# Moving the folded-row sums of a Fourier-and-mixer kernel: three batches' steps put into other slots

## The chip, the cores and the metric

The kernel runs on one core of one Trainium2 chip. The metric is the device time of one execution in microseconds. TensorE (PE) does the matrix products, VectorE (DVE) and ScalarE (ACT) do elementwise work and read PSUM, GpSimd (POOL) does small copies and gathers, SyncE (SP) issues most transfers.

## The reference

For `x` of shape (8, 3136, 256), in float32:

```python
X = np.fft.fft(x, axis=1)
X = np.fft.fft(X, axis=2)
x = X.real                                  # the first part

xt = x.transpose(0, 2, 1)                   # the second part
h  = xt @ U @ V                             # U: 3136 x 32, V: 32 x 3136
u  = x + h.transpose(0, 2, 1)
ch = np.maximum(u @ w_ch1, 0.0) @ w_ch2     # 256 -> 1024 -> 256
out = u + ch
```

So each batch of 3136 rows goes through a two-dimensional Fourier transform, of which the real part is kept, then a rank-32 mix along the rows, then a two-layer product along the columns, with the residual added.

## The kernel before

**Two streams of work.** The transform of a batch works on folded rows: by the symmetries of sine and cosine, rows (and columns) are added to and subtracted from their mirror images first, and the products then need only a quarter of the terms. The second part works on chunks of 512 rows out of the first half of each batch (1568 rows; eight batches make 25 chunks, `c` from 0 to 24) together with their mirror rows (`hf` 1). While the chunks of one batch go through the second part, the next batch is transformed, and the one after that is folded. Batch 0 is transformed at the start, in an order written out by hand.

**The fold of a batch** (`fold`, all on VectorE through `fold_tt`, line 453 in the profile) has these steps: for the even and then the odd quarters, `along_d` adds and subtracts columns of the forward rows (`eof` from the loaded `xf`) and of the reversed rows (`eor` from `xr`), in two parts each; `load_part` then loads the next batch into `xf` and `xr` (two gathers issued by GpSimd, one transfer by SP, and small ones); `mirror` sums the two into `eos`, in two parts. At the end `half` and `fourth` make `ge`, `gc` (even rows) and `go` (odd rows), which the products read. Batch 1 has 13 steps, batches 2 to 6 have 17, batch 7 has 15. GpSimd copies two columns beside them (`alone`).

**The transform of a batch** (`transform`) has these steps, each of them products on TensorE and what reads them: `a` and `s` are the even rows (`even_rows`: a first product, a ScalarE copy `ev`, a second product into the same PSUM tile, ScalarE copies into A or B, then VectorE's `mirrored`, line 635); `c` and `d` are the odd rows (`seq`: the first product is copied to `ev` by ScalarE and halved into `eh` by VectorE; the second is joined with `eh` by VectorE in `join`, lines 584 to 598, into A or B). In the text `a0`, `a1`, `c0` and so on are the first and second of each. Types `a`, `c` make A, types `s`, `d` make B. `chan` multiplies A and B along the columns and copies the result into S (`h` 0) or T (`h` 1); `lowrank`, `hidden` and `spread_rank` make the rank-32 factors.

**The chunks.** In chunk `c`, `direct` multiplies `u` by the first weights (four tiles `p1` at a time, ScalarE's activations of line 845), `mirrors` turns the same tiles into those of the mirror rows (line 861), `second_product` multiplies by the second weights into a tile `p2` and VectorE adds `u` (lines 923, 924), `store` writes `o` out, and `front` makes the next `u`: two small products `ph` and two VectorE sums with S and T (line 458), then a transposing transfer on SP. `odd_part` makes `uo`.

**PSUM.** The tiles `p1` have four buffers, `p2` two, and all of the transform's tiles and the two `ph` of a front share the two buffers with the tag `dft`.

**What sets the order.** A chunk has places called slots, numbered 6c + 0 to 6c + 5 with some in between (4.5, 4.75). `turn(c, sl)` runs the steps that are due there. `put` fills the table: for each batch, first the fold's steps at the slots in `FOLDS` (or at `mid` - 18 + n), and then the transform's steps from slot `mid` on, one list for each slot. `mid` is 11 for batch 1, 23 for batch 2, and 39, 57, 75, 93, 111 for batches 3 to 7. Products and folds are pinned to program order among themselves; joins, copies and `o` sums are placed by the scheduler's own estimate of the times. Line 1145 puts the seventh list of batch 1 at slot 16.5.

Of the kernel before, what the change touches and what calls it, by code (L numbers as in the profile page):

```python
# [31 lines left out]
def kernel(  # L32
# [9 lines left out]
    nc = tc.nc  # L42
    B, S, D = x.shape
# [413 lines left out]
    def in_turn(c, *a, **k):  # L457
        ins = nc.vector.tensor_tensor(*a, **k)  # L458
        if pinned and c <= 2:
            tc.keep_in_program_order(ins)  # L460

    def mm(*a, **k):
        ins = nc.tensor.matmul(*a, **k)  # L463
        if len(pinned) > 1:
            tc.keep_in_program_order(ins)
        if pinned:
            pinned.append(ins)
# [185 lines left out]
        nc.scalar.copy(ST[b]["tab"][:, typ, 0, :].rearrange("p (g r) -> p g r", r=R),  # L653
                       four(kept["pt"][:], typ * R))

    def chan(b, ch, h, tag="dft"):
        d = ST[b]
        at, n0 = ((0, 0), (785, 1), (393, 786), (1177, 785))[ch]
        n = 393 if ch == 0 else 392
        if b == 0 and ch == 2:  # L660
            at, n0, n = 392, 784, 393
        pt = psum.tile([P, TE], FP32, tag=tag, name="pst", bufs=BUFS[tag])
        mm(pt[:, :n], MC[:, h * P:(h + 1) * P], d["A"][:, at:at + n], start=True, stop=False)
        mm(pt[:, :n], (MSX if ch == 3 and b == 0 else MSN)[:, h * P:(h + 1) * P], d["B"][:, at:at + n],
           start=False, stop=True)
        to = d["ST"[h]][:, n0:n0 + 2 * n - 1:2]
        if b == 0 and h == 1:
            nc.vector.tensor_copy(to, pt[:, :n])
        else:
            nc.scalar.copy(to, pt[:, :n])  # L670

    def lowrank(b):
        d = ST[b]
# [78 lines left out]
    def spread_rank(b):  # L752

        (nc.scalar if b == 1 else nc.sync).dma_start_transpose(out=QF[b % 2][:], in_=QT[:])

    def width(c):
        return min(CH, NCOL - c * CH)

    def pieces(c):

        cuts = []
        r = c * CH
        while r < c * CH + width(c):
            b, n = divmod(r, HALF)
            end = min(c * CH + width(c) - b * HALF, HALF)
            cuts.append((b, n, end, r - c * CH))
            r = b * HALF + end
        return cuts
# [3 lines left out]
    def front(c, hf):  # L772

        k = CK.setdefault(c, {})
        first = hf == 1 and c in DIRECT
        u = cp.tile([P, 2 * CH // P + first, P], BF16, tag="ut1" if first else f"u{hf}", name=f"u{hf}",
                    bufs=2 if first else 2 - hf)
        u = k["u", hf] = u[:, 0:2 * CH // P].rearrange("p (s t) m -> p s (t m)", s=2)
        phs = [psum.tile([P, CH], FP32, tag="dft", name="ph", bufs=BUFS["dft"]) for s in range(2)]
        w = width(c)  # L780
        if w < CH:
            nc.gpsimd.memset(u[:, :, w:].bitcast(I32), 0)
        for b, lo, hi, col in pieces(c):
            at, v = (w - col - hi + lo, S - hi + 1) if hf else (col, lo)
            for s in range(2):
                rows = slice((2 * hf + s) * R, (2 * hf + s + 1) * R)
                mm(phs[s][:, at:at + hi - lo], TA[b % 2][rows, s * P:(s + 1) * P], VV[rows, v:v + hi - lo],
                   start=True, stop=True)
        for s in range(2):
            for b, lo, hi, col in pieces(c):  # L790
                src = ST[b]["S" if s == hf else "T"]
                if hf == 0:
                    at, src = col, src[:, lo:hi]
                else:
                    at = w - col - hi + lo
                    if lo == 0:
                        nc.vector.tensor_tensor(u[:, s, w - col - 1:w - col], phs[s][:, w - col - 1:w - col],
                                                src[:, HALF:HALF + 1], op=AL.add)
                        lo = 1
                    src = src[:, hi - 1:lo - 1:-1] if lo else src[:, hi - 1::-1]  # L800
                in_turn(c, u[:, s, at:at + hi - lo], phs[s][:, at:at + hi - lo], src, op=AL.add)
        if hf == 1:
            for b, lo, hi, col in pieces(c):
                if lo == 0:
                    nc.gpsimd.tensor_copy(UH[:, :, b], u[:, :, w - col - 1])
                    nc.gpsimd.tensor_copy(UH[0:1, :, b], u[0:1, ::-1, w - col - 1])
        else:
            if w < CH:
                nc.gpsimd.tensor_copy(u[:, :, w:w + B], UH[:])
        if c in DIRECT:  # L810
            return
        n = CH // P
        ut = k["ut", hf] = cp.tile([P, 2 * n + 1, P], BF16, tag=f"ut{hf}", name=f"ut{hf}", bufs=2)
        nc.gpsimd.memset(ut[:, 2 * n, 0:2], 0.0)
        nc.sync.dma_start_transpose(out=ut[:, 0:2 * n], in_=u.rearrange("p s r -> p (s r)"))
        fx = k["fx", hf] = cp.tile([P, n, 2], FP32, tag=f"fx{hf}", name=f"fx{hf}", bufs=2)
        if hf:
            nc.gpsimd.tensor_tensor(fx[:, :, 0], ut[:, n:2 * n, 0], ut[:, 0:n, 0], op=AL.subtract)
        nc.gpsimd.tensor_tensor(fx[:, :, 1], ut[:, 0:n, 0] if hf else ut[:, n:2 * n, 0],  # L819
                                ut[:, n + 1:2 * n + 1, 0], op=AL.subtract)  # L820
# [109 lines left out]
    def transform(b):  # L930

        def odd_rows(typ, pn):
            seq(b, 1, typ, pn)
            if pn:
                join(b, 1, typ)

        def even(typ, pn):
            even_rows(b, typ, pn)
            if pn:
                mirrored(b, typ, ST[b])  # L940

        a = [lambda pn=pn: even(1, pn) for pn in range(2)]
        s = [lambda pn=pn: even(0, pn) for pn in range(2)]
        c = [lambda pn=pn: odd_rows(1, pn) for pn in range(2)]
        d = [lambda pn=pn: odd_rows(0, pn) for pn in range(2)]
        rank = [lambda: lowrank(b)]
        ch = [lambda ch=ch, h=h: chan(b, ch, h) for ch in range(2) for h in range(2)]
        q = [lambda: hidden(b)]
        if b == 1:
            return 11, [a[:1], c[:1] + a[1:], c[1:] + s[:1], s[1:] + d[:1], d[1:] + ch[:1], ch[1:3],  # L950
                        rank + ch[3:] + q + [lambda: spread_rank(b)]]
        if b == 2:
            return 23, [a[:1], a[1:] + c[:1], [], c[1:] + s[:1], s[1:], d[:1], d[1:], ch[:1], ch[1:2] + rank,
                        q, ch[2:3], ch[3:]]
        return 6 * (b * HALF // CH) - 15, [[x] for x in a + c + d[:1] + s + d[1:] + ch[:1] + rank + ch[1:2] + q + ch[2:]]
# [173 lines left out]
    def put(slot, *steps):  # L1129
        due.setdefault(slot, []).extend(steps)  # L1130

    FOLDS = {1: (5, 5, 6, 6, 6, 7, 8, 8, 9, 9, 10, 10, 12),
             2: (15, 15, 15, 16, 16, 17, 17, 18, 18, 19, 20, 20, 21, 21, 21, 22, 22.75),
             3: (27, 27, 29, 30, 30, 31, 31, 32, 33, 33, 34, 34, 35, 35, 36, 37, 38)}
    for b in range(1, B):
        mid, steps = transform(b)
        todo = list(fold(b))
        places_ = FOLDS.get(b) or [mid - 18 + n for n in
                                   ((1, 2, 3, 5, 5, 6, 6, 8, 9, 10, 11, 11, 12, 13, 14, 15, 17) if b + 1 < B else
                                    (1, 2, 3, 5, 6, 6, 8, 9, 10, 11, 12, 13, 14, 15, 17))]  # L1140
        assert len(todo) == len(places_)
        for step, at in zip(todo, places_):
            put(at, step)
        for n, step in enumerate(steps):
            put(16.5 if mid + n == 17 and b == 1 else mid + n, *step)
# [4 lines left out]
    def turn(c, sl):  # L1150
        for step in due.get(6 * c + sl, []):
            step()
# [30 lines left out]
    for c in range(1, NCH):  # L1183
        direct(c, 0)
        if c > 1:
            odd_part(c)
        turn(c, 0)
        second_product(c - 1, 0, 2, between=lambda: turn(c, 1))
        store(c - 1, 0)
        mirrors(c, 0)  # L1190
        front(c, 1)
        second_product(c - 1, 1, 0)
        turn(c, 2)
        direct(c, 1)
        turn(c, 3)
        second_product(c - 1, 1, 2, between=lambda: turn(c, 4))
        store(c - 1, 1)
        turn(c, 4.5)
        mirrors(c, 1)
        if c + 1 < NCH:  # L1200
            front(c + 1, 0)
        turn(c, 4.75)
        second_product(c, 0, 0)
        turn(c, 5)
# [38 lines left out]
```

## Time and profile before

| | us |
|---|---|
| median of 3 runs | 442.1 (442.1 to 442.47) |
| the profiled execution | 441.79 |
| its span, first to last instruction | 440.0 |
| TensorE busy | 422.8 (96%) |
| VectorE busy | 318.6 (72%) |
| ScalarE busy | 293.0 (67%) |
| GpSimd busy | 136.2 (31%) |

In the rows of a timeline the first number is the start in us from the span's start, the second how long it took, then engine, line, operation, the tile written and the tiles read, their shapes, and how many instructions are merged. A bracket at the end gives the idle time of that engine just before, and who ended it. Matrix products are pipelined, so neighbours overlap by some 0.15 us. All products stand on line 463, all folds on line 453, since helpers issue them.

### The profile page before, as it was taken

To read this page: it belongs to the slowest core of one execution; us is meant where nothing else is said; L and a number is where in the kernel's file an instruction comes from. 1 tells how busy PE (TensorE), PEld (TensorE's weight loads), DVE (VectorE), ACT (ScalarE), POOL (GpSimd) and SP (SyncE) were. 2 spreads that over 40 slices of the span, in tenths; PEclk is the share of its full clock that TensorE was granted. 3 is DMA by queue.
4 is the path that set the end of the run, shared out by engine and by line. 5 is a ranking of instruction groups with operands and counts; after the bars stand their busy time and mean duration, and the time that the engine had idled before them with its cause. 6 is when DMAs were issued, how large, how long until landed. Compare 5 with 4: busy or idle time off the path is not lost.

```text
span 440.0 us, 9349 instructions
## 1 busy us (share of the span) xinstructions
PE 422.8 (96%) x3457; PEld 283.9 (65%) x3504; DVE 318.6 (72%) x663; ACT 293.0 (67%) x635; POOL 136.2 (31%) x340
## 2 busy tenths in 40 slices
PE   5989999999999999999999999999999999999996
PEld 2764666666666666667666666667666766666675
DVE  8988985997799778759867778769867554353442
ACT  7958765666667757766667757766667757765651
POOL 8871331571214144423253232332132100111111
PEclk9999999999999999999999999999999999999999
DMA  7898698479399766925886386776234423434544
GB/s 194 215 224 191 153 276 107 132 217 243 101 199 255 118 153 177 252 73 151 197 168 203 101 208 74 184 188 134 65 97 126 114 75 95 103 113 127 121 119 125
DMA packets 89166, 67.83 MB, mean 154 GB/s; under 512 B 55403, under 2 KB 82431, under 8 KB 89119
## 3 DMA queue, kind: packets, MB, share of 16 engines
q1 hardware_dynamic: 83350, 52.79, 50.0%
q0 software_dynamic: 5472, 14.36, 12.8%
q8 instruction: 27, 0.44, 0.4%
q14 instruction: 21, 0.16, 0.1%
q10 hardware_dynamic: 296, 0.07, 0.1%
HBM read 28.86 MB, written 25.69 MB: 124 GB/s over the span
## 4 chain that ended last, share of the span: by engine, by line
PE 80%; ACT 7%; DVE 6%; DMA 2%; POOL 2%; issue 2%; SPq 1%; ACTq 0%
PE p L463 65%; PE pt L463 7%; PE pst L463 4%; ACT h L845 3%; PE ph L463 2%; DMA xr<-in_x_dram 2%; DVE eos L453 1%; PE ptt L463 1%; ACT h L861 1%; ACT S L670 1%; DVE B L584 1%; PE pq L463 1%; DVE B L590 1%; ACT ev L616 1%; SPq L87 1%
## 5 line engine op out<-in xcount | busy, mean ns | idle before, releaser
L463 PE MATMUL p<-w,h 128*128 128x256 bf16 x1576 | 195.1, 273 | 0.0
L463 PEld LDWEIGHTS <-h 128*128 128x128 bf16 x1576 | 148.7, 98 | 40.5 <-issue 16.5
L861 ACT ACTIVATE h<-p 128x512 bf16<-128x512 f32 (+1 forms) x200 | 101.5, 595 | 83.1 <-PE p L463 77.8
L845 ACT ACTIVATE h<-p 128x512 bf16<-128x512 f32 (+1 forms) x200 | 101.8, 600 | 8.5 <-PE p L463 8.0
L928 POOL TENSOR_TENSOR o<-o,fx 128x2 f32<-128x2 f32 (+1 forms) x95 | 48.3, 508 | 151.4 <-DVE o L924 83.7
L463 PE MATMUL p<-u,w 128*128 128x512 bf16 (+1 forms) x354 | 90.4, 374 | 3.0 <-ACT u L725 0.5
L923 DVE TENSOR_TENSOR o<-p,ut 128x256 f32<-128x256 f32 (+1 forms) x95 | 39.6, 416 | 64.4 <-PE p L463 44.1
L463 PEld LDWEIGHTS <-w 128*128 128x128 bf16 x512 | 41.8, 97 | 38.1 <-issue 1.8
L463 PE MATMUL p<-uo,wd 128*128 128x512 bf16 (+1 forms) x199 | 50.6, 375 | 0.3
L57 POOL DMA_INDIRECT xf<-in_x_dram,xidx x32 | 37.0, 1157 | 20.5 <-DVE eof L453 10.3
L458 DVE TENSOR_TENSOR u<-ph,T 128x512 bf16<-128x512 f32 (+23 forms) x63 | 34.3, 555 | 10.2 <-PE ph L463 8.2
L924 DVE TENSOR_TENSOR o<-p,ut 128x256 f32<-128x256 f32 (+1 forms) x95 | 38.8, 409 | 0.0
L453 DVE TENSOR_TENSOR eof<-xf 99x1016 bf16<-99x1016 f32 (+1 forms) x33 | 38.2, 1170 | 0.8 <-DMA xf<-in_x_dram,xidx 0.8
L453 DVE TENSOR_TENSOR eor<-xr 99x1016 bf16<-99x1016 f32 (+1 forms) x34 | 38.4, 1141 | 0.0
L458 DVE TENSOR_TENSOR u<-ph,S 128x512 bf16<-128x512 f32 (+23 forms) x63 | 34.2, 553 | 1.3 <-PE ph L463 0.8
L819 POOL TENSOR_TENSOR fx<-ut 128x4 f32<-128x4 bf16 x48 | 14.7, 306 | 49.8 <-DMA ut<-u 49.7
L463 PEld LDWEIGHTS <-wd 128*128 128x128 bf16 x200 | 19.4, 98 | 13.1 <-issue 0.4
L463 PE MATMUL pt<-te,gc 98*128 98x229 bf16 (+1 forms) x192 | 24.0, 260 | 0.7 <-ACT ev L616 0.5
L670 ACT CAST S<-pst 128x392 bf16<-128x392 f32 (+1 forms) x30 | 18.6, 621 | 6.7 <-PE pst L463 6.4
L463 PEld LDWEIGHTS <-gc 98*128 98x128 bf16 x216 | 19.4, 97 | 5.1 <-issue 1.1
L463 PE MATMUL ph<-vv,ta 32*128 32x512 bf16 (+15 forms) x126 | 20.4, 324 | 1.6 <-DVE tab L598 0.8
L670 ACT CAST T<-pst 128x392 bf16<-128x392 f32 (+1 forms) x28 | 17.3, 617 | 6.9 <-PE pst L463 6.8
(178 smaller groups left out, 446.6 us busy)
## 6 DMA issues: line engine op xcount, KB each, us to landing
out_dram<-o SPq DMA_DIRECT2D x33, 512.0 KB
xr<-in_x_dram SPq DMA_DIRECT2D x15, 784.0 KB
out_dram<-o SPq DMA_DIRECT2D x8, 384.0 KB
out_dram<-o SPq DMA_DIRECT2D x8, 256.0 KB
out_dram<-o SPq DMA_DIRECT2D x10, 128.0 KB
xr<-in_x_dram SPq DMA_DIRECT2D x2, 392.0 KB
ut<-u SPq DMA_TRANSPOSE x48
vv<-vv SPq DMA_DIRECT2D x3, 196.0 KB
```

The source lines that it names most:

```text
L57: nc.gpsimd.indirect_dma_start(out_, None, bass.AP(t.tensor, t.offset, [[w, rows], [1, w]]), bass.IndirectOffsetOnAxis(idx, 0), element_of ...
L87: return [lambda dst=dst, dims=dims, at=at: (eng or nc.sync).dma_start(out=dst, in_=bass.AP(t.tensor, lo + at, dims)) for dst, dims, at in ...
L453: ins = nc.vector.tensor_tensor(*a, **k)
L458: ins = nc.vector.tensor_tensor(*a, **k)
L463: ins = nc.tensor.matmul(*a, **k)
L670: nc.scalar.copy(to, pt[:, :n])
L819: nc.gpsimd.tensor_tensor(fx[:, :, 1], ut[:, 0:n, 0] if hf else ut[:, n:2 * n, 0], ut[:, n + 1:2 * n + 1, 0], op=AL.subtract)
L845: nc.scalar.activation(k["h", 0][q][:, j - 4 * q, :w], p1[:, :w], AF.Relu)
L861: nc.scalar.activation(k["h", 1][q][:, g, :w], k["p1"][g][:, :w][:, ::-1], AF.Relu)
L923: nc.vector.tensor_tensor(o[:, ts, 0:P], p2[:, :w, 0:P], ut[:rows, ts, 0:P], op=AL.add)
L924: nc.vector.tensor_tensor(o[:, ts, P:D], p2[:, :w, P:D], strip(ut[:rows], (CH // P + t0 + 1) * P, [[P, w], [-1, P]]), op=AL.add)
L928: nc.gpsimd.tensor_tensor(o[:, ts, cols], o[:, ts, cols], fx[:rows, ts, 1 - hf:], op=AL.add)
```

## The change

Five edits:

- Batch 1's transform: `c1` and `d0` stand in slot 13, `s0`, `d1`, `s1` in slot 14 (before: `c1`, `s0` in 13, `s1`, `d0` in 14, `d1` and a `chan` in 15). The four `chan` steps go second channel first: the two of `h` 0 in slot 15, copied by VectorE instead of ScalarE (a new argument `eng`), the two of `h` 1 in slot 16. The rank steps follow at 16.5; no `chan` stands among them any more.
- Batch 1's last fold step (`half(1, 1)`, which makes `go`) goes from slot 12 to 10.75.
- Batch 2's first two folds go from slot 15 to 13 and 13.75 (a new `turn(c, 1.75)` between `front(c, 1)` and `second_product(c - 1, 1, 0)`, where only this step is ever due), its first load of batch 3 from 16 to 15, and some later folds by up to one slot.
- Batch 3's first two folds go from slot 27 to 26, its third from 29 to 30.
- Batches 4 to 7: the two sums `mirror(0)` go from slot `mid` - 12 to `mid` - 13, that is from behind `direct(c, 1)` to ahead of it.

```diff
-    def chan(b, ch, h, tag="dft"):
+    def chan(b, ch, h, tag="dft", eng=None):
 ...
-        if b == 0 and h == 1:
-            nc.vector.tensor_copy(to, pt[:, :n])
-        else:
-            nc.scalar.copy(to, pt[:, :n])
+        eng = eng or (nc.vector.tensor_copy if b == 0 and h == 1 else nc.scalar.copy)
+        eng(to, pt[:, :n])
 ...
         if b == 1:
-            return 11, [a[:1], c[:1] + a[1:], c[1:] + s[:1], s[1:] + d[:1], d[1:] + ch[:1], ch[1:3],
-                        rank + ch[3:] + q + [lambda: spread_rank(b)]]
+            return 11, [a[:1], c[:1] + a[1:], c[1:] + d[:1], s[:1] + d[1:] + s[1:],
+                        [lambda ch=ch: chan(b, ch, 0, eng=nc.vector.tensor_copy) for ch in (1, 0)], [ch[3], ch[1]],
+                        rank + q + [lambda: spread_rank(b)]]
 ...
-    FOLDS = {1: (5, 5, 6, 6, 6, 7, 8, 8, 9, 9, 10, 10, 12),
-             2: (15, 15, 15, 16, 16, 17, 17, 18, 18, 19, 20, 20, 21, 21, 21, 22, 22.75),
-             3: (27, 27, 29, 30, 30, 31, 31, 32, 33, 33, 34, 34, 35, 35, 36, 37, 38)}
+    FOLDS = {1: (5, 5, 6, 6, 6, 7, 8, 8, 9, 9, 10, 10, 10.75),
+             2: (13, 13.75, 15, 15, 15, 16, 16, 17, 18, 19, 20, 20, 20, 21, 21, 22, 22.75),
+             3: (26, 26, 30, 30, 30, 31, 31, 32, 33, 33, 34, 34, 35, 35, 36, 37, 38)}
 ...
-                                   ((1, 2, 3, 5, 5, 6, 6, 8, 9, 10, 11, 11, 12, 13, 14, 15, 17) if b + 1 < B else
-                                    (1, 2, 3, 5, 6, 6, 8, 9, 10, 11, 12, 13, 14, 15, 17))]
+                                   ((1, 2, 3, 5, 5, 5, 5, 8, 9, 10, 11, 11, 12, 13, 14, 15, 17) if b + 1 < B else
+                                    (1, 2, 3, 5, 5, 5, 8, 9, 10, 11, 12, 13, 14, 15, 17))]
 ...
         front(c, 1)
+        turn(c, 1.75)
         second_product(c - 1, 1, 0)
```

## The prediction

> **What bounds the kernel now.** I read the page first, then busy time in stretches, then the waits of TensorE, then the timelines of TensorE and VectorE at each place where TensorE stood still.
>
> ```profile
> PE 422.8 (96%) x3457; PEld 283.9 (65%) x3504; DVE 318.6 (72%) x663; ACT 293.0 (67%) x635; POOL 136.2 (31%) x340
> ```
> ```profile
> 64.00:78.00 14.00, 12.92 (x103) 8.65 (x102) 8.87 (x21) 7.84 (x20) 1.69 (x10) 1.00 0.72 118
> 78.00:92.00 14.00, 13.20 (x127) 8.91 (x127) 13.57 (x27) 9.21 (x20) 9.06 (x6) 1.00 0.68 172
> ```
> TensorE (PE) is busy 96% of the 440.0 us span, so only its pauses can be won. The columns of the stretches are PE, its weight loads, VectorE, ScalarE, GpSimd. From 64 to 78 us (batch 1's transform) VectorE works 8.87 of 14 us, and then it is full: 13.57 of 14. Work moved from the second stretch to the first has 5.1 us to go into.
>
> ```profile
> PE ph L463 <- DVE tab L598: 0.8, 4, 0.2
> PE pq L463 <- ACT T L670: 0.7, 1, 0.7
> PE pst L463 <- DVE tab L598: 0.6, 2, 0.3
> PE pt L463 <- DVE go L453: 0.3, 1, 0.3
> ```
> These are TensorE's waits in the main loop that matter. All but the last are waits for one of the two `dft` buffers in PSUM, held by a tile that another engine has not yet read. A wait in this view is shorter than what it costs, because an early product's drain counts as busy. I therefore take the cost from starts: the time between two starts, less the time the same products take elsewhere.
>
> **The change, part by part.** Batch 1 first:
>
> ```profile
> 63.04 0.57 PE L463 MATMUL pt<-ts,go 98*128 98x228 bf16 x4 [0.26 <-DVE go L453]
> ...
> 67.16 1.03 PE L463 MATMUL p<-uo,wd 128*128 128x512 bf16 x4
> ...
> 68.36 0.38 PE L463 MATMUL ph<-vv,ta 32*128 32x512 bf16 x1
> 69.51 0.37 PE L463 MATMUL ph<-vv,ta 32*128 32x512 bf16 x1 [0.78 <-DVE u L458]
> 69.82 1.92 PE L463 MATMUL p<-w,h 128*128 128x256 bf16 x16
> 71.57 0.96 PE L463 MATMUL pt<-te,gc 98*128 98x229 bf16 x8
> ...
> 75.41 0.33 PE L463 MATMUL pst<-A,mc 128*128 128x393 bf16 x1
> ...
> 75.74 1.03 PE L463 MATMUL p<-w,h 128*128 128x256 bf16 x8
> 76.61 0.33 PE L463 MATMUL pst<-A,mc 128*128 128x393 bf16 x1
> ...
> 77.36 0.34 PE L463 MATMUL pst<-A,mc 128*128 128x392 bf16 x1 [0.24 <-DVE tab L598]
> ...
> 79.21 0.33 PE L463 MATMUL pst<-A,mc 128*128 128x392 bf16 x1
> ...
> 80.44 0.55 PE L463 MATMUL pq<-tl,w 128*128 128x32 bf16 x16 [0.73 <-ACT T L670]
> ```
> ```profile
> 363.22 0.38 PE L463 MATMUL ph<-vv,ta 32*128 32x512 bf16 x2
> 363.53 1.92 PE L463 MATMUL p<-w,h 128*128 128x256 bf16 x16
> ```
> ```profile
> 61.75 1.23 DVE L453 TENSOR_TENSOR go<-eos 99x2064 bf16<-99x2064 bf16 x1
> ...
> 64.84 0.60 DVE L635 SCALAR_TENSOR_TENSOR A<-ev,pt 128x392 bf16<-128x392 f32 x1
> ```
> *GO earlier (slot 12 to 10.75).* `half(1, 1)` goes ahead of two `o` sums and `uo`, about 1.2 us earlier, so the 0.26 us before 63.04 goes. It pushes those three back by its own length, to about 63 us; the next reader, `mirrors` with `uo`, starts at 67.16. What is late next: the odd products `d0`, which now follow `c1` and need the buffer that the mirrored sum at 64.84 frees at 65.44. They would be ready about 0.25 us sooner than that. I book 0.
>
> *Odd rows around the sums of u.* Before, `s0` opens a tile in slot 13 that stays open over the front products `ph`, which must then share one buffer: 68.36 to 69.82 is 1.46 us, where an undisturbed pair takes 363.53 - 363.22 = 0.31. Cost 1.15. After, slot 13 holds `c1` and `d0`, whose tiles are read at once (`d0` by one ScalarE copy), and `s0`, `d1`, `s1` stand together in slot 14. Both buffers should be free at `ph`: gain 1.15.
>
> *Two channel copies on VectorE, order of `chan`.* 76.61 + 0.33 (a pair of channel products, 75.41 to 75.74) = 76.94, but the next starts at 77.36: 0.42 lost to the buffer of `d1`'s join. After, `s1` stands between `d1` and the chans, and eight front products more, so the join is done: gain 0.42. The copies themselves:
>
> ```profile
> L668 DVE CAST T<-pst x2: 593/595/597, 38.3 to 42.4; 128x393 bf16<-128x393 f32 x1, 128x392 bf16<-128x392 f32 x1
> ```
> ```profile
> 79.40 0.21 ACT L684 CAST tl<-ptt 128x64 bf16<-128x64 f32 x1 [0.90 <-PE ptt L463]
> ```
> Two copies of 0.6 us, free of ScalarE's four activations. After the last chan, `hidden` starts at 80.44 where 79.21 + 0.33 = 79.54 was possible: 0.90 lost. In the new order both second-half chans come before the rank products, with eight products of `p` between, so the buffer is no longer the matter. What is late next is `hidden`'s own input: the rank products drain, and TL is copied in 0.21 us. I estimate 0.44 for drain and copy (between 0.21 and the 0.90 of now), and book 0.46.
>
> *Folds of batch 2 sooner.* Two `eof` folds move to slots 13 and 13.75, about 2.3 us of VectorE ahead of the joins of `d`. By adding durations as an estimate, VectorE then runs from 65 to 74 us nearly without a break: from the mirrored sum's end at 65.3 come the join and `d0`'s halves (1.8), a fold (1.2), two `o` sums (0.7) and the front's first sum (0.6), so to 69.5, some 0.35 us before `s0` wants that sum's buffer; and `d1`'s join starts about when its products end. So it costs 0 by my order, and up to 1.2 (one fold, below) if one lands ahead of the join. Load of batch 3 (`load_part(3, 0)`, two gathers on GpSimd, one transfer on SP) goes from slot 16 to 15, still right behind the last fold that reads its buffers; queued behind it on SP is the store of the chunk, which moves up with it. Batch 1: 1.15 + 0.42 + 0.46 = 2.03 us.
>
> Batch 2:
>
> ```profile
> 97.17 1.92 PE L463 MATMUL p<-w,h 128*128 128x256 bf16 x16
> 99.31 0.56 PE L463 MATMUL pt<-te,gc 98*128 98x229 bf16 x4 [0.22 <-DVE u L458]
> ...
> 114.91 1.92 PE L463 MATMUL p<-w,h 128*128 128x256 bf16 x16
> 116.93 0.92 PE L463 MATMUL pt<-to,go 98*128 98x424 bf16 x6
> ...
> 119.91 1.04 PE L463 MATMUL p<-w,h 128*128 128x256 bf16 x8
> 121.27 0.34 PE L463 MATMUL pst<-A,mc 128*128 128x393 bf16 x1 [0.32 <-DVE tab L598]
> ```
> ```profile
> 117.73 1.21 DVE L453 TENSOR_TENSOR eor<-xr 99x1016 bf16<-99x1016 f32 x1
> ```
> Sixteen `p` products take 71.57 - 69.82 = 1.75, eight take 76.61 - 75.74 = 0.87. So 0.39 is lost at 99.31, 0.27 at 116.93 and 0.49 at 121.27. The first goes because VectorE, full from 78 us, starts that stretch with two folds already done. The second: batch 3's two `eof` folds move from slot 27 to 26, into the pause ahead of the mirrored sum of B. The third: the `eor` fold at 117.73, which stood ahead of `d1`'s join, moves from slot 29 to 30, behind it. Gain 1.15.
>
> Batches 4 to 7 (sums `mirror(0)` from slot mid-12 to mid-13):
>
> ```profile
> 214.71 0.37 PE L463 MATMUL ph<-vv,ta 32*128 32x512 bf16 x1
> 215.28 0.38 PE L463 MATMUL ph<-vv,ta 32*128 32x512 bf16 x1 [0.20 <-DVE tab L598]
> 215.60 1.59 PE L463 MATMUL p<-w,h 128*128 128x256 bf16 x13
> ```
> ```profile
> 208.46 1.21 DVE L453 TENSOR_TENSOR eor<-xr 99x1016 bf16<-99x1016 f32 x1
> 211.84 0.60 DVE L635 SCALAR_TENSOR_TENSOR B<-ev,pt 128x392 bf16<-128x392 f32 x1 [2.17 <-ACT tab L622]
> 212.33 1.29 DVE L453 TENSOR_TENSOR eos<-eof,eor 99x1024 bf16<-99x1024 bf16 x2
> ...
> 214.95 0.27 DVE L598 CAST tab<-pt 1x128 bf16<-1x128 f32 x1
> ```
> The pair of `ph` takes 215.60 - 214.71 = 0.89 against 0.31: 0.58 lost, since `d1`'s tile is read out only at 215.22. VectorE idles 2.17 us before 211.84 and then runs 1.2 us of `eos` sums ahead of the join. Moved to slot mid-13, the sums follow the `eor` fold of 208.46 and end near 210.9, inside that pause. The join then starts as `d1`'s products end and is over about 0.1 us before `ph` wants the buffer. This happens four times (the view of waits counts 4), 4 x 0.58 = 2.32. The pair at 363.22, in batch 7's transform, is the kernel's own control: no folds follow it, and it does not wait.
>
> Sum: 2.03 + 1.15 + 2.32 = 5.5 us. The profiled execution took 441.79 us (span 440.0), so 436.3; the median of the runs is 0.3 above, so 436.6 us.
>
> **The rivals.**
>
> *The folds overtake the copies.* At slot 15 the two `eor` folds may be placed ahead of the two VectorE copies, as 117.73 shows the scheduler doing to a join that waits for TensorE. The copies come 2 x 1.2 us later, and the second-half chans, which need their buffers, some 1.8 later. For: that row. Against: there a join was not yet ready, here the first copy is ready as the second's products are issued. Time: 436.6 + 1.8 = 438.4.
>
> *The bubble is a shortage of buffers.* The wait of `ph` comes back every batch. If two buffers are simply too few there, an earlier join only changes who holds them, the four waits stay, and the time is 436.6 + 2.3 = 438.9. Against it stands the pair at 363.22, which runs with the same two buffers; for it, that I left only 0.1 us. The Trainium skill, Perfetto Trace Analysis, section Identifying the Most-Contended Engine, says that a gap which repeats on the engine that should be saturated can mean too little SBUF or PSUM for the next tile; by it the cure would be another buffer, and not the sums' place, and the pair at 363.22 does not agree.
>
> *The scheduler keeps its order in batches 1 and 2.* Joins and `o` sums are not pinned; if it fills the gaps otherwise there, only the four waits go: 442.1 - 2.3 = 439.8. If the sums stay behind the mirrored sum as well, the change does not do what it says: 442.1.
>
> *SP's queue, slower.* The load of batch 3 starts near 78 instead of 82 us, beside the store and the next transpose.
>
> ```profile
> 60.66 8.36 SPq L815 DMA_TRANSPOSE ut<-u  x1
> ```
> Here one transpose held SP's queue for 8.36 us. If this happens again at 78 us, stores come late, VectorE waits for an `o` buffer, `p2` stays full, and TensorE stops. If all of it reached TensorE the time would be 436.6 + 8.4 = 445.0; it decides once over 6.4 us reach it. For: that row. Against: at 60.66 itself TensorE lost next to nothing to it, and the DMA share from 64 to 92 us is about 0.7.
>
> **How the numbers follow.** About 0.9 us, 0.2%, is what a measurement of this kernel can tell from no change. Chances: all parts as summed, within about 1 us, 0.50; the folds overtake 0.13; the shortage 0.12; only the four waits 0.08; nothing moves 0.07; SP's queue or another stop of that size 0.10. Faster 0.83, same 0.07, slower 0.10. The range goes from 435.6 (1 us of pauses beyond my sum) to 440.2, which takes in the first four cases and leaves out 0.17 above it. All parts alone would give 435.6 to 437.6.
>
> **What would show it.** TensorE's waits for `tab` L598 at `ph` gone in all four batches, `eos` sums ending before the mirrored sum of B; `ph` in batch 1 back to a pair at about 67.8 us; the products of `hidden` near 78.4 instead of 80.44; batch 2's `pst` without its wait. A step is wrong where its wait is still there, or where TensorE waits at `s0`, at `ch[3]`, or for a VectorE copy S. The forecast as a whole is wrong if these pauses go and the end does not come sooner by their sum: then something else than TensorE sets the end.

## The result, and the profile after

The changed kernel takes 440.06 us (median, 439.66 to 440.81 in 6 runs) against 442.1 us (441.5 to 442.97 in 6 runs): a ratio of 0.9953 with an interval of 0.994 to 0.9966. The forecast was 436.6 us. The direction was right; 2.0 us came where 5.5 were summed.

The profiled execution of after is the slowest of its six: 440.81 us, span 439.0, so its losses are a little larger than those of the median. Line numbers from 670 to 945 are two lower in it than in before, so before's 923 is 921; the changed kernel with the cut store, below, has 923 again. First the page's row of busy time and the same two stretches as in the prediction:

```profile
PE 422.1 (96%) x3457; PEld 284.1 (65%) x3504; DVE 319.9 (73%) x665; ACT 292.2 (67%) x633; POOL 139.8 (32%) x340
```
```profile
64.00:78.00 14.00, 12.22 (x97) 8.06 (x96) 11.66 (x24) 6.41 (x16) 4.53 (x11) 1.00 0.86 155
78.00:92.00 14.00, 13.37 (x126) 8.83 (x126) 11.70 (x26) 9.09 (x21) 3.91 (x6) 1.00 0.86 185
```

VectorE's work went where it was sent: 8.87 and 13.57 us of the two stretches became 11.66 and 11.70. But TensorE's busy time in the first fell from 12.92 to 12.22 us: it now stands longer there. The waits of TensorE say where (waited for, us in total, times, longest):

```profile
PE pst L463 <- DVE tab L598: 1.6, 1, 1.6
PE pst L463 <- DVE u L458: 1.5, 4, 0.4
...
PE pq L463 <- ACT tl L682: 0.3, 1, 0.3
PE p L463 <- DVE u L458: 0.3, 1, 0.3
```

All four waits of before that the prediction quoted are gone (`ph` on `tab`, `pq` on `T`, the two short ones of `pst` on `tab`, `pt` on `go`). The wait for `tl` is the one that was forecast behind the rank products. The other three rows are new and were not forecast, and each can be found in the timelines. TensorE of after:

```profile
58.01 0.38 PE L463 MATMUL ph<-vv,ta 32*128 32x512 bf16 x2
...
67.38 0.38 PE L463 MATMUL ph<-vv,ta 32*128 32x512 bf16 x2
...
71.95 1.89 PE L463 MATMUL p<-u,w 128*128 128x512 bf16 x7
75.40 0.34 PE L463 MATMUL pst<-A,mc 128*128 128x392 bf16 x1 [1.56 <-DVE tab L598]
...
79.74 0.43 PE L463 MATMUL pq<-tl,w 128*128 128x32 bf16 x11 [0.30 <-ACT tl L682]
...
84.20 1.67 PE L463 MATMUL p<-u,w 128*128 128x512 bf16 x7 [0.27 <-DVE u L458]
```
```profile
164.23 0.38 PE L463 MATMUL ph<-vv,ta 32*128 32x512 bf16 x2
164.54 1.92 PE L463 MATMUL p<-w,h 128*128 128x256 bf16 x16
166.83 0.33 PE L463 MATMUL pst<-A,mc 128*128 128x393 bf16 x1 [0.37 <-DVE u L458]
```

Both front products are a pair again, at 67.38 and at 164.23, as forecast. Then TensorE stops behind them: at 75.40, where the seven `p` products from 71.95 should have led to 73.7 (1.89 us less the overlap of 0.15); and at 166.83, where sixteen `p` products from 164.54 should have led to 166.29. The second stop is 0.54 us and the pair had lost 0.58, so the exchange is nearly even. VectorE of after shows what stood ahead each time:

```profile
69.60 1.20 DVE L453 TENSOR_TENSOR eof<-xf 99x1016 bf16<-99x1016 f32 x1
72.99 0.42 DVE L921 TENSOR_TENSOR o<-p,ut 128x256 f32<-128x256 f32 x1 [2.19 <-PE p L463]
...
73.66 0.56 DVE L584 TENSOR_TENSOR B<-pt,eh 128x392 bf16<-128x392 f32 x1
```
```profile
159.10 1.30 DVE L453 TENSOR_TENSOR eos<-eof,eor 99x1024 bf16<-99x1024 bf16 x2
161.36 0.60 DVE L635 SCALAR_TENSOR_TENSOR B<-ev,pt 128x392 bf16<-128x392 f32 x1 [0.95 <-ACT tab L622]
162.36 0.57 DVE L584 TENSOR_TENSOR B<-pt,eh 128x392 bf16<-128x392 f32 x1 [0.41 <-PE pt L463]
...
164.65 0.40 DVE L458 TENSOR_TENSOR uo<-S,T 128x512 bf16<-128x512 bf16 x1
164.98 1.20 DVE L453 TENSOR_TENSOR eof<-xf 99x1016 bf16<-99x1016 f32 x1
166.10 0.67 DVE L458 TENSOR_TENSOR u<-ph,S 128x512 bf16<-128x512 f32 x1
```

The same steps in before, first VectorE, then the first `ph` on TensorE:

```profile
164.03 0.56 DVE L584 TENSOR_TENSOR B<-pt,eh 128x392 bf16<-128x392 f32 x1
...
166.31 0.67 DVE L458 TENSOR_TENSOR u<-ph,S 128x512 bf16<-128x512 f32 x1
...
167.50 0.40 DVE L458 TENSOR_TENSOR uo<-S,T 128x512 bf16<-128x512 bf16 x1
167.84 1.20 DVE L453 TENSOR_TENSOR eof<-xf 99x1016 bf16<-99x1016 f32 x1
```
```profile
165.20 0.37 PE L463 MATMUL ph<-vv,ta 32*128 32x512 bf16 x1
```

In batch 1 an `o` sum waits 2.19 us, and the join of `d1` is queued behind it. The releaser named there, a product, cannot be right: the sum stays idle long after that product. In batches 3 to 6 the join does come sooner, as forecast; but the room that this leaves ahead of the sums of `u` is filled by an `eof` fold of 1.20 us (164.98), which is put ahead of `u`. In before the order was the two sums of `u` (166.31 and right behind it), `uo`, `eof`. The sums of `u` free the `dft` buffers that the channel products `pst` need. In batch 1 the same happens at 81.61, where an `eof` fold delays `u`, and TensorE stops for 0.27 us at 84.20 with a first part just before it.

### The profile page after: what moved, and what is told of

It is laid out like the page before. It is cut to its first block, busy times and chain, and to the rows that moved or that the text cites. A ratio compares the mean times of both kernels' runs of the same rounds, so it can differ in the third digit from the quotient of the medians.

```text
span 439.0 us, 9351 instructions
## 1 busy us (share of the span) xinstructions
PE 422.1 (96%) x3457; PEld 284.1 (65%) x3504; DVE 319.9 (73%) x665; ACT 292.2 (67%) x633; POOL 139.8 (32%) x340
## 4 chain that ended last, share of the span: by engine, by line
PE 87%; DVE 4%; ACT 3%; DMA 2%; POOL 2%; issue 1%; POOLq 0%; ACTq 0%
PE p L463 71%; PE pt L463 7%; PE pst L463 5%; PE ph L463 2%; DMA xf<-in_x_dram,xidx 2%; ACT h L843 1%; POOL xf L57 1%; DVE eof L453 1%; PE ptt L463 1%; DVE u L458 1%; PE pq L463 1%; DVE eor L453 1%; DVE eos L453 1%; ACT h L859 0%; POOL em L283 0%
## 5 line engine op out<-in xcount | busy, mean ns | idle before, releaser
L817 POOL TENSOR_TENSOR fx<-ut 128x4 f32<-128x4 bf16 x48 | 17.7, 369 | 53.5 <-DMA ut<-u 53.4
L463 PE MATMUL pst<-A,mc 128*128 128x392 bf16 (+1 forms) x60 | 19.8, 330 | 3.2 <-DVE tab L598 1.6
L668 ACT CAST S<-pst 128x392 bf16<-128x392 f32 (+1 forms) x28 | 17.4, 620 | 6.1 <-PE pst L463 6.0
```

The costliest lines, as they stand in the source:

```text
L668: eng(to, pt[:, :n])
```

## The experiments

Theory: TensorE's pauses were priced rightly, and removed, but two things that the forecast held fixed took the gain back: the scheduler's place for the `eof` fold (four times 0.55 us, and about 0.6 in batch 1), and an `o` sum that waits for a store (about 1 us). The rivals: TensorE is held by two buffers whatever the order; or the rest of the change is worth nothing.

**The `o` sum.** It writes one of two `o` buffers, so it waits until the store that last read that buffer has landed. That store holds 127 rows. The first run cuts it into 112 and 15:

```diff
+            for q0, q1 in (((0, 112), (112, np_)) if np_ == 127 else ((0, np_),)):
-                nc.sync.dma_start(... row * D, [[D, np_], ...]), in_=o[p:p + np_, ...])
+                nc.sync.dma_start(... (row + q0) * D, [[D, q1 - q0], ...]), in_=o[p + q0:p + q1, ...])
```

> The changed kernel, with the store of 127 rows (the first piece of a mirror chunk at a batch's start, 127 x 256 in float32) cut into one of 112 rows and one of 15; nothing else. Theory S (store): the o sum that sits 2.19 us late at 72.99 us waits for the landing of that store, which frees its o buffer; it holds VectorE's queue, with the join of d1 behind it, and TensorE's 1.6 us wait at 75.40 is its price. Cut, the sum starts near 71, the wait at the chan is gone, and the time is about 438.2 us against 440.1 (1.5 to 2 us less). Rival T (TensorE): the sum waits for a product, as the view of waits names it; the cut changes nothing, 440.1.

439.1 us (438.65 to 440.68), ratio 0.9934 (0.9917 to 0.9951): 1.0 us less than after on the median, where 1.9 were expected. VectorE no longer stands:

```profile
71.31 1.21 DVE L453 TENSOR_TENSOR eof<-xf 99x1016 bf16<-99x1016 f32 x1
72.44 0.42 DVE L923 TENSOR_TENSOR o<-p,ut 128x256 f32<-128x256 f32 x1
```

The sum follows the fold directly, and the wait of `pst` on `tab` is gone. Between the two profiled executions the expected 1.9 is there: from the front products ahead of the change to `hidden` TensorE takes 21.73 us in after (58.01 to 79.74) and 19.85 here (59.72 to 79.57). This profiled execution is the slowest of its six all the same, since TensorE waited 1.49 us in it at 24.07, ahead of everything that the cut touches. The median has only half of the 1.9. What the stop costs differs between traces: in that of the next run, which has the whole store too, the same stretch takes 20.96 us (58.41 to 79.37), 1.12 more than the 19.84 with both edits below. The same cut on the kernel before is the control:

> The kernel before, with the store of 127 rows cut into 112 and 15 rows. Theory S: there the sum that needs the buffer started at 71.77 us, when its products had just ended (71.73) and the store had just landed (71.63), so the store is hidden and the cut changes nothing: 442.1, within 0.5. If the store also feeds other waits (the transposing transfer that holds SP's queue for 8.36 us at 60.66), 440 to 441.

441.98 us (441.24 to 443.8), ratio 0.9999 (0.9987 to 1.0012): no difference. There the products of `d1` come later, so nothing is queued behind the sum that matters.

**The sums of `u`.** `in_turn` keeps the sums of `u` and `uo` at their written place only in chunks up to 2. From chunk 3 on they are placed by the scheduler, as joins, copies and `o` sums are, which the account of the order ahead of the prediction leaves out. Now they are kept in all:

```diff
-        if pinned and c <= 2:
+        if pinned:
```

> The changed kernel, with the front's u sums and uo kept in program order among the folds in all chunks (before: in chunks 0 to 2 only). Theory O (order): in batches 3 to 6 the wait of ph was not removed but moved, because the scheduler now puts an eof fold of 1.2 us ahead of the front's u sums, which hold both dft buffers; the chan behind them waits 0.37 us and loses 0.55, four times, and in batch 1 direct(3, 0) loses 0.6 in the same way. With the u sums first, these are gone: about 2.2 + 0.6 less, 437.3 us. Rival B (buffers): two dft buffers are too few there, and the wait moves on to a third place; 439.5 to 440.1.

437.09 us (436.43 to 437.9), ratio 0.9885 (0.9868 to 0.9903): 2.97 us less than after, as expected within 0.2. The waits for `u` are gone, and the time from one join of `d1` to the next is 48.92 us in place of 49.50. Both edits together:

> The changed kernel with both edits, the cut store and the u sums in program order. If theories S and O hold, their gains add, since they lie at different places: 440.1 - 1.9 - 2.8 = about 435.4 us, close to the 436.6 that was forecast for the change alone. If only one holds, 437 to 438; if none, 440.1.

436.08 us (435.98 to 436.56), ratio 0.9868 (0.9851 to 0.9886). The two gains add: 0.96 + 2.97 = 3.93, and 440.06 - 436.08 = 3.98. This is the best kernel of the study. VectorE in batch 4's steps, now with the fold behind `u`:

```profile
162.20 0.68 DVE L458 TENSOR_TENSOR u<-ph,S 128x512 bf16<-128x512 f32 x1
162.80 0.68 DVE L458 TENSOR_TENSOR u<-ph,T 128x512 bf16<-128x512 f32 x1
...
164.77 1.21 DVE L453 TENSOR_TENSOR eof<-xf 99x1016 bf16<-99x1016 f32 x1
```

**The moved sums of batches 4 to 7 by themselves**, on the kernel before, without and with `u` in turn, and `u` in turn alone:

```diff
-   ((1, 2, 3, 5, 5, 6, 6, 8, ...) if b + 1 < B else (1, 2, 3, 5, 6, 6, 8, ...))
+   ((1, 2, 3, 5, 5, 5, 5, 8, ...) if b + 1 < B else (1, 2, 3, 5, 5, 5, 8, ...))
```

> The kernel before with one edit of the change alone: the sums of the first mirror rows of batches 4 to 7 go from position 6 of their chunk to position 5. Theory (the order of the sums of u took back what these sums gave): in batches 3 to 6 one pair wait of ph of 0.58 us goes, and one wait of pst on u of about 0.5 us appears, because an eof fold is put ahead of the sums of u; period from one d1 join to the next 49.5 us as before, time 442.0 us, within 0.4 of the kernel before. The forecast's own step: 4 x 0.58 = 2.32 us less, 439.7 us. Rival (the sums of u came late in the changed kernel because of its other edits): no wait of pst on u, 439.7 us as well.

> The same edit, and the sums of u and the copies uo keep their written place in every chunk, not in chunks up to 2 alone. Theory: neither the ph wait nor the pst wait is left in batches 3 to 6, period 48.9 us in place of 49.5, so 4 x 0.58 = 2.3 us below the next kernel: about 439.5 us. Rival (TensorE is held by two ps buffers, whatever the order): 442 us, a wait of the same length in another place of the period.

> The kernel before, with the sums of u and the copies uo kept in their written place in every chunk, and nothing else. Theory: in batches 3 to 6 they stood ahead of the eof fold already, so the four pair waits of ph stay, the period stays 49.5 us, and the time is that of the kernel before, 441.4 to 442.2 us; what differs can only be in chunks 3 to 5. Rival (the kept place is worth its time by itself, and the gain that it brought on the changed kernel has nothing to do with the moved sums): about 439.1 us.

| kernel | median us | ratio to before | join to join, us |
|---|---|---|---|
| sums only | 441.75 (441.34 to 443.02) | 0.9993 (0.9977 to 1.0009) | 49.51 |
| sums, `u` in turn | 439.69 (438.73 to 444.57) | 0.9938 (0.9918 to 0.9959) | 48.93 |
| `u` in turn only | 441.49 (440.93 to 445.12) | 1.0 (0.9979 to 1.002) | 49.51 |

Neither edit alone does anything that these runs can tell; together they bring 2.4 us on the median of before (442.1). The shorter period gives 4 x 0.58 = 2.32 of it. That the two agree so closely is partly luck, since keeping `u` and `uo` in turn does two more things on before's places, in both kernels that have it. It removes the pause of 0.49 us at batch 2's channel products (the second pair now starts 0.88 and 0.87 us after its eight products do, which is what eight take). And it brings a new stop, because `uo` now stands behind an `o` sum that waits for a store: TensorE waits 0.4 us for `uo` in the trace of the last kernel. In that of the middle one, which is its slowest execution, 444.57 us, it waits until 106.67 us, and the row of waits is:

```profile
PE p L463 <- DVE uo L458: 2.9, 1, 2.9
```

In the kernel with the sums alone, TensorE's rows show the same exchange as in after, so none of the other edits causes it:

```profile
165.56 0.38 PE L463 MATMUL ph<-vv,ta 32*128 32x512 bf16 x2
...
168.16 0.33 PE L463 MATMUL pst<-A,mc 128*128 128x393 bf16 x1 [0.37 <-DVE u L458]
```

And undone, on the kernel of 436.08 us:

> The changed kernel with the 127-row store cut and the sums of u in turn everywhere (436.08 us), and the sums of the first mirror rows of batches 4 to 7 put back to where the kernel before had them. Theory (with u in turn these sums are worth the forecast's 4 x 0.58 us): the four pair waits of ph come back, period 49.5 us in place of 48.9, 438.4 us. Rival (they are worth nothing on this kernel either, and the whole gain is that of the kept place of u): 436.1 us.

438.31 us (437.98 to 438.46), 2.2 more. The pair splits again:

```profile
161.76 0.37 PE L463 MATMUL ph<-vv,ta 32*128 32x512 bf16 x1
162.33 0.39 PE L463 MATMUL ph<-vv,ta 32*128 32x512 bf16 x1 [0.20 <-DVE tab L598]
```

The rival of too few buffers has fallen: with the same two buffers the pause goes or stays by order alone.

**The folds of batches 2 and 3**, back to before's places on the kernel of 436.08 us:

```diff
-             2: (13, 13.75, 15, 15, 15, 16, 16, 17, 18, 19, 20, 20, 20, 21, 21, 22, 22.75),
-             3: (26, 26, 30, ...
+             2: (15, 15, 15, 16, 16, 17, 17, 18, 18, 19, 20, 20, 21, 21, 21, 22, 22.75),
+             3: (27, 27, 29, ...
```

> The same kernel of 436.08 us, with the folds of batches 2 and 3 at the positions of the kernel before. Theory (the forecast's three steps of batch 2): 0.4 us lost again at the even products near 99 us, 0.3 at the odd products near 117, 0.5 at the channel products near 121, so 1.1 to 1.2 more: 437.2 us. Rival (batch 1's new order alone leaves VectorE room, the earlier folds add nothing): 436.1 us.

437.81 us (436.99 to 438.27): 1.7 more, but not where expected. Of the three terms only the 0.3 at the odd products came back whole; 0.1 came back at the even products and nothing at the channel products. Most of the loss is a new stop, seen on TensorE and VectorE:

```profile
102.80 1.04 PE L463 MATMUL p<-uo,wd 128*128 128x512 bf16 x4 [1.05 <-DVE uo L458]
```
```profile
101.58 0.42 DVE L923 TENSOR_TENSOR o<-p,ut 128x256 f32<-128x256 f32 x1 [2.97 <-DMA out_dram<-o]
...
102.33 0.41 DVE L458 TENSOR_TENSOR uo<-S,T 128x512 bf16<-128x512 bf16 x1
```

Again an `o` sum waits for a store, with the pinned `uo` behind it: the stop of the two kernels above that pin `uo` on before's places. So 1.7 is the worth of this set of places in this kernel; it doesn't price the forecast's three terms one by one. With only the first two `eof` folds put back:

```diff
-             2: (13, 13.75, 15, 15, 15, 16, ...
+             2: (15, 15, 15, 15, 15, 16, ...
```

> The same kernel of 436.08 us, with only batch 2's first two eof folds back at position 15. Theory (the forecast's first step of batch 2): VectorE, full from 78 us, starts that stretch 2.4 us further behind, and the first 0.4 us of batch 2 is lost again: 436.5 us. Rival (two folds ahead of batch 1's joins cost what they bring): 436.1 us or less.

437.86 us (437.24 to 437.93): 1.8 more, where the theory had 0.4. The two folds now stand behind batch 1's copies of S, and VectorE reaches the sums of `u` for chunk 3 late:

```profile
82.57 0.39 PE L463 MATMUL p<-u,w 128*128 128x512 bf16 x1 [0.69 <-DVE u L458]
83.23 1.67 PE L463 MATMUL p<-u,w 128*128 128x512 bf16 x7 [0.27 <-DVE u L458]
```

From the small `ph` products of chunk 3 to the channel products behind them it takes 5.10 us here (79.64 to 84.74) and 3.80 in the kernel of 436.08 us (79.74 to 83.54): 1.3 us. The even products of batch 2, where the forecast's 0.4 was to return, lose nothing. The two profiled spans differ by about this, 435.5 against 434.3 us; the rest of the 1.8, some 0.6, is in no trace.

**VectorE's copies of S**, put back on ScalarE:

```diff
-                        [lambda ch=ch: chan(b, ch, 0, eng=nc.vector.tensor_copy) for ch in (1, 0)], ...
+                        [lambda ch=ch: chan(b, ch, 0) for ch in (1, 0)], ...
```

> The changed kernel with the store of 127 rows cut into 112 and 15 and the sums of u in turn everywhere (436.08 us), and batch 1's two copies of S that the change gave to VectorE put back on ScalarE, at their new place. Theory: they queue there behind the activations of the same chunk and reach TensorE later: a ph wait of 0.4 to 1 us in batch 1, 436.4 to 437.1 us. Rival (TensorE has other products to do until then): no new wait, 436.1 us.

436.48 us (435.88 to 436.7) against 436.08 (435.98 to 436.56): the ranges overlap, so these runs don't decide. The profile shows the order that the theory names, though: the copies start at 75.14 behind four activations on ScalarE, and at 74.51 on VectorE. The `ph` wait that it expected is not there; from the front products to `hidden` TensorE takes 20.17 us in place of 19.84, and what is lost lies at the channel products.

## Why the prediction was right and where it failed

The kernel of 436.08 us keeps the whole change and takes away the two things that the forecast had not seen. Each of its two edits alone does nothing to the time of before (441.98 and 441.49 us). Its starts can be set against before's, step by step. Its rows:

```profile
58.31 0.38 PE L463 MATMUL ph<-vv,ta 32*128 32x512 bf16 x2
...
78.15 0.55 PE L463 MATMUL pq<-tl,w 128*128 128x32 bf16 x16 [0.30 <-ACT tl L682]
...
96.64 0.57 PE L463 MATMUL pt<-te,gc 98*128 98x229 bf16 x4
...
114.00 0.92 PE L463 MATMUL pt<-to,go 98*128 98x424 bf16 x6
...
117.85 0.33 PE L463 MATMUL pst<-A,mc 128*128 128x393 bf16 x1
```

And of after, the last three of these places:

```profile
98.91 0.56 PE L463 MATMUL pt<-te,gc 98*128 98x229 bf16 x4
...
116.30 0.92 PE L463 MATMUL pt<-to,go 98*128 98x424 bf16 x6
...
120.29 0.34 PE L463 MATMUL pst<-A,mc 128*128 128x393 bf16 x1
```

Before's starts less these give what each step brought; the first is the start of the change's region, and its difference is no part of it. In before it is this row:

```profile
58.42 0.38 PE L463 MATMUL ph<-vv,ta 32*128 32x512 bf16 x2
```

The last line takes the spans, 440.0, 439.0 and 434.3.

| step | forecast | after | both taken away |
|---|---|---|---|
| batch 1, up to `hidden` (80.44) | 2.03 | 0.70 - 0.41 = 0.29 | 2.29 - 0.11 = 2.18 |
| even products of batch 2 (99.31) | 0.39 | 0.40 - 0.70 = -0.30 | 2.67 - 2.29 = 0.38 |
| odd products (116.93) | 0.27 | 0.63 - 0.40 = 0.23 | 2.93 - 2.67 = 0.26 |
| channel products (121.27) | 0.49 | 0.98 - 0.63 = 0.35 | 3.42 - 2.93 = 0.49 |
| batches 4 to 7 | 2.32 | 1.0 - 0.98 = 0.0 | 5.7 - 3.42 = 2.3 |

- **TensorE's pauses and their price:** right. Every term stands in the last column within 0.15 us, and 436.08 us lies 0.5 from the forecast's 436.6. The two missed waits are worth 3.98 us together, a little more than the 3.5 by which the change fell short. The 0.15 comes from the early `go`, booked at 0: the products that wait for it gained 0.43, and the mirrored sum behind it, which the forecast named, took back 0.27. That the whole sum comes so near is partly luck, as two of batch 2's terms show below.
- **Batches 4 to 7, the failed step, 2.32 us.** The `eos` sums do end inside VectorE's pause (159.10 to 160.39) and the join is over ahead of `ph`, as forecast. What the step lacked is what runs next: it took the order of VectorE behind the join as before's. The join now starts 1.87 us ahead of the first `ph` (162.36 to 164.23), in before 1.17 (164.03 to 165.20); the scheduler filled the room with a fold, and the first sum of `u` starts 1.87 us behind that `ph` (166.10) and not 1.11 (166.31). Shown by the three kernels on before and by the undoing: 0 alone, 2.3 with `u` in turn. Why the scheduler chose that place for the fold is not shown.
- **Batch 1, "it costs 0 by my order".** The forecast priced a fold ahead of `d1`'s join, up to 1.2 us. The fold came at 69.60 and was over in time; what held the join was the `o` sum after it. In before this sum starts at 71.77, and the join stood well behind it. The change brought the join forward to where the landing of a store decides: about 1.0 us on the median. (The prediction's rows put the mirrored sum's end at 65.44 and not 65.3, and its durations add to 69.6 and not 69.5; neither changes a term.) A second fold ahead of `u` in chunk 3 took 0.58 more in after (0.70 us ahead at 79.74, 0.12 at 85.71), which stands in the table's second line.
- **Batch 2's three terms.** The first was right in size and wrong in its reason: with the two early folds put back the even products still lose nothing, and 1.3 us go at chunk 3's `u` instead. Its size was luck too: in the five traces with before's batch 1 this pause is between 0.05 and 0.88 us, in the eight with the changed one at most 0.11; which part of batch 1's change removes it was not tried. The second's reason stands: with the folds back 0.28 us are lost there again. The third, 0.49, comes in the last column from `u` in turn as well, since that alone removes the pause on before; the moved fold without it brought 0.35 in after.
- **The rivals.** "The folds overtake the copies" named the right actor in the wrong place: folds were put ahead of the sums of `u`, not of the copies of S. "The bubble is a shortage of buffers" fell by the order alone. The sentence of the Trainium skill that the prediction cites for it stands in Perfetto Trace Analysis under the next heading, "Optimization Strategy"; it says that such a gap can mean too little SBUF or PSUM, and here it did not. "SP's queue" pointed at the row of the transpose, 8.36 us at 60.66, and dismissed it at its own place. The effect that it named, VectorE waiting for an `o` buffer, came there, at 72.99; but what the `o` sum waits for is the landing of the store just ahead of the transpose. The store's cut shortens the transpose too; on before that made no difference, and whether the long transpose costs TensorE anything in after was not tried by itself.

## What to carry to other kernels

A pause that is removed moves the whole queue behind it: after moving a step, write down the next three instructions of that engine in their new order, and ask of each that a scheduler may place whether something ready will be put ahead of it. Where the order matters, pin the consumer that frees the buffer, and not only the producer that was moved: here neither edit was worth anything alone, and both 2.4 us. A pin has its price as well: whatever stands behind it waits for the slowest step ahead, as `uo` did behind the `o` sum. And list the elementwise steps that wait for a store's landing; one that is covered by a pause today is next in line when the pause goes.

## What the runs showed of the hardware

The store of 127 rows runs on one DMA engine. Bandwidth in 40 slices of 0.5 us from 56 to 76 us, first after, then the kernel with both taken away:

```profile
GB/s 334 367 442 373 226 231 198 125 216 153 81 289 344 205 197 262 211 350 317 281 162 41 25 23 104 198 29 25 23 25 25 25 25 148 325 387 389 296 285 9
```
```profile
GB/s 309 356 395 455 322 259 217 210 158 148 126 397 238 170 256 168 322 400 353 317 262 173 205 110 0 4 0 0 350 385 344 288 207 0 0 139 221 352 139 115
```

In after a tail of 23 to 29 GB/s, broken once near 68.5, runs on to 72.5 us; with the cut it is gone by 68. In that tail the trace's packets of 1024 bytes, one row of the store each, start 0.04 us apart and take 0.046 each, so they go nearly one after another. The store was issued at 58.07 us and its semaphore's last mark is at 72.87, 0.12 before the `o` sum starts; cut, the parts issued at 58.40 and 58.92 have landed by 67.73. In one trace (the moved sums with `u` in turn) the profile names the store itself, where other traces name a product:

```profile
72.65 0.42 DVE L923 TENSOR_TENSOR o<-p,ut 128x256 f32<-128x256 f32 x1 [2.09 <-DMA out_dram<-o]
```

The Trainium skill, "DMA: Bandwidth & Descriptors", section "Why a DMA increments its semaphore by 16 and not by 1", says that a transfer issued like this one spreads over the largest number of engines, up to 16, that divides the slowest dimension on both of its sides, and that for 127 partitions this is one; the semaphore is raised at once for the engines not used. The trace agrees: that semaphore has marks at 58.6 and 72.87 only; that of the part with 112 rows has 16 marks between 67.32 and 67.51, and that of the 15 rows one at 59.65 and 15 from 67.54 to 67.73.

The transpose behind the store on SP also changed. First after, then the kernel with both taken away:

```profile
60.24 10.02 SPq L813 DMA_TRANSPOSE ut<-u  x1
```
```profile
60.55 2.96 SPq L813 DMA_TRANSPOSE ut<-u  x1
```

In the six kernels with the whole store it holds SP's queue for 8.4 to 10.0 us, in the seven with the cut store for 1.9 to 3.0. Why it holds the queue longer behind the whole store was not tried.

In one trace a long stop of TensorE cost more than its length. In the execution of 444.57 us the granted clock is 0.50 from 106.01 us, inside the stop that ends at 106.67, to 112.84, and 1.00 on both sides. Sixteen `p` products take 3.38 us there (109.46 to 112.84) in place of 1.75. By the starts the stop itself is 3.04 us (103.63 to 106.67), and from 101.88 to 112.84 TensorE takes 10.96 us where the kernel of 436.08 us takes 5.01 (99.56 to 104.57) for the same products. After the shorter stops in this document, of 1.7 us and less, the clock was 1.00.
